# Fused attention with head mixing and a gated MLP: sooner loads of the values into a fourth buffer, one gate store split in two, two more matmul units held back

## The chip, the cores and the metric

The kernel runs on one core of one Trainium2 chip. A core has five engines with queues of their own: TensorE for matmuls (PE in the profile, its weight loads PEld), VectorE (DVE), ScalarE (ACT), GpSimd (POOL) and SyncE (SP, which here only issues DMAs). POOL issues DMAs too. The engines run independently; an instruction waits until what it needs has been signalled, and what stands behind it on the same engine waits with it. The metric is the time of one execution in microseconds (us), as the median of several runs; lower is better.

## The reference

Attention over 8 batches, 12 heads, 448 positions and head size 64, with a 12x12 mix of the heads before and after the softmax, then a two-layer MLP on all 3584 tokens (768 to 2048 to 768) whose gate is `h - tanh(h)`. Cut to what is computed:

```python
def _attn_ref(q, k, v, w_pre, w_post):
    scores = scale * np.matmul(q, k.transpose(0, 1, 3, 2))
    scores = np.einsum('bhij,hg->bgij', scores, w_pre)
    scores = scores - np.max(scores, axis=-1, keepdims=True)
    attn = np.exp(scores)
    attn = attn / (np.sum(attn, axis=-1, keepdims=True) + 1e-09)
    attn = np.einsum('bhij,hg->bgij', attn, w_post)
    return np.matmul(attn, v)

def _moe_ref(x, w_in, w_out):      # x: the 3584 x 768 result of attention
    h = x @ w_in
    g = h - np.tanh(h)
    return g @ w_out
```

## The kernel before

**Attention, about the first 860 us.** A batch is cut into four blocks of 120, 120, 120 and 88 query rows (32 blocks), and each block into groups of ten rows (45 groups a batch). The loop runs over 180 *places* `p`; each takes two groups: `premix` mixes the scores over the heads (tile `ps_p` from the gathered scores `t`), `expo` takes the maximum `mx` and the exponential `e`, `norm` makes the weights `wr` on POOL one place later, and `mix` multiplies `e` by `wr` (`ps_o`, copied to `at`). Beside that a table `todo` says which other jobs a place does: `prep_k` and `prep_q` (transposes), `scores` (`ps_q`, copied to `s`), and `values(i, t)`, which multiplies half of the heads of block `i` of the mixed attention `at` by the values `vr` (`ps_m`).

The values of a batch come in three tiles `vr` of four heads each (`hq` 0, 1, 2; 448 KB a tile). `values(i, 0)` reads tiles 0 and 1, `values(i, 1)` tiles 1 and 2. Three buffers serve all batches, so a new tile overwrites the tile with the same number of the batch before. A job `load_v(b, hq)` in the table puts the transfer on a list; at the next place SP first issues that place's gathers (`gather`, the scores `s` of two groups, read back into `t` for the place after next), and then up to six of the listed transfers, in order. Among them are also the keys `kr`, the queries `qr`, the results of attention `xs`, and the traffic of a conversion that runs beside attention: `cr` loads a piece of the MLP's weights, DVE, ACT and POOL split it, and `wi<-co`, `ss<-ct`, `wo<-co`, `ts<-ct` store it. SP is one queue: a transfer that must wait holds up all behind it.

**The MLP.** The 3584 tokens are seven blocks of 512. The first goes through plain products. The other six go in three pairs (`s` = 0, 1, 2) by a scheme that needs seven products where eight would be plain (Strassen's): `pair_step` makes seven products (`ps_h`) for one of eight pieces `q` of the hidden size, and the gates' results, in seven combinations, are stored to DRAM in `gss[s]`, slots 0 to 6, by POOL. The class `Late` does the gates of a piece in steps `v0` to `v5`, spread over the next piece's products: `v0` stores slots 0 and 1 (from `ga`), `v3` and `v4` make the second gate `gb` (the last write is the masked copy of L328), and `v5` forms the sums and stores slots 2 and 3 (from `gb`, L669) and 4 to 6 (from `gs`, L670). In `gb[:, 1]` stands the plain second gate, which is slot 3; `v5` writes only `gb[:, 0]`.

The output products are cut into *units* of twelve matmuls (`seventh`, L530 to L532: tile `y` from gates and weights). A generator (`Results.run`) yields them in a fixed order: for each `s` the slots in the order 3, 1, 6, 5, 0, 4, 2, each with `k` = 0, 2, 4, 6, and two units for each `k`. One `k` needs a gate tile of 512 KB read back from `gss[s]` (`gl<-gs`, SP, L402; in the last stretch also into free tiles such as `b22l` and `t3l`) and a weight tile of 768 KB (`w<-wo` or into `b22h`, `t4h` and others, L392 and L395). The load for `k` = 6 of any slot needs the stores of the pieces `q` = 6 and 7.

Units of one pair are mixed into the pair steps of the next (`share`). After the eighth pair step of a pair a number of units runs alone, while `Late` of the last piece is worked off, one step after every second unit (L1356 to L1367). How many is set by

```python
    HELD, AHEAD, FIRST = (14, 14, 10), (2, 4, 4), (4, 6, 5)
```

`HELD[s]` units of what was left from before are held back for that stretch, and `AHEAD[s]` units of the pair's own follow in it. After the last pair step of `s` = 2 these are 10 and 4; then the generator runs to its end with no other work beside it. The number of units in a pair step is what is left without `HELD` and `FIRST`, spread evenly.

Of the kernel before, what the change touches and what calls it, by code (L numbers as in the profile page):

```python
# [10 lines left out]
F32 = mybir.dt.float32  # L11
# [137 lines left out]
def kernel_body(  # L149
# [11 lines left out]
    nc = tc.nc  # L161
    B, H, S, D = q.shape
# [3 lines left out]
    NP = H // 2  # L166
    CP = 112
    NC = S // CP
# [29 lines left out]
    gss = [dram.tile([P, 7, NQ, TB], F32, name=f"gs{x}", tag=f"gs{x}") for x in range(NS)]  # L198
# [53 lines left out]
    def work(tag, n=2):  # L252
        return (ff.hid if tag in ("h01", "h23") else ff.rw).tile([P, n, TB], F32, name=tag, tag=tag)
# [381 lines left out]
    class Late:  # L635
# [23 lines left out]
        def v4(self):  # L659
            self.gs = work("gs", 3)  # L660
            self.g2.d4(self.gb)
            nc.vector.tensor_add(self.gs[:, 0:2], self.ga, self.gb[:, 0].unsqueeze(1).to_broadcast([P, 2, TB]))

        def v5(self):
            nc.vector.scalar_tensor_tensor(
                out=self.gs[:, 2], in0=self.ga[:, 1], scalar=-1.0, in1=self.gs[:, 0], op0=ALU.mult, op1=ALU.subtract
            )
            nc.vector.tensor_sub(self.gb[:, 0], self.gb[:, 1], self.gs[:, 2])  # L668
            nc.gpsimd.dma_start(gss[self.s][:, 2:4, self.q], self.gb)  # L669
            nc.gpsimd.dma_start(gss[self.s][:, 4:7, self.q], self.gs)  # L670
            ff.stored[self.s] = self.q + 1

# [63 lines left out]
    with ExitStack() as st:  # L736
# [7 lines left out]
        kp = st.enter_context(tc.tile_pool(name="kp", bufs=1, side="right"))  # L744
# [14 lines left out]
        def dma(dst, src, to=None):  # L759
            entry = [place[0], dst, src, None]  # L760
            (queue if to is None else to).append(entry)
            return lambda places=0: entry[3] is not None and entry[3] + places <= place[0]
# [19 lines left out]
            krs[b, hq] = t  # L782

        def load_v(b, hq):
            t = kp.tile([CP, 4, NC, D], F32, name="vr", tag="vr", bufs=3)
            sent[b, hq, "v"] = dma(
                t.rearrange("p h c d -> p h (c d)"),
                v[b, 4 * hq : 4 * hq + 4].rearrange("h (p c) d -> p h (c d)", c=NC),
            )
            vts[b, hq] = t  # L790
# [254 lines left out]
        for hq in range(3):  # L1045
            load_v(0, hq)
# [101 lines left out]
        def at_place(p, *job):  # L1148
            todo[p].append(job)

        halved = []
        for i in range(len(blocks)):
# [7 lines left out]
                    halved.append((e if i else x - 1, hi, "s", i + 1, x))  # L1160
            for x in range(2):
                halved.append(((f1 - 1) // 2 + 2, f2 // 2 + 1 if f2 < NG else NPL + 7, "v", i, x))
        at_s, p, kind = {}, 0, None
        window = {i: (lo, hi) for lo, hi, k, i, _ in sorted(halved, reverse=True) if k == "s"}
        while halved:
            ready = sorted((x for x in halved if x[0] <= p), key=lambda x: (x[1], x[3:]))
            if ready:
                x = ready[0]
                assert p <= x[1], (p, x)

                other = [y for y in ready if y[2] != kind]
                if x[2] == kind and other and x[1] > p + 1:
                    x = other[0]
                halved.remove(x)
                _, _, kind, i, n = x
                if kind == "s":
                    at_s[i, n] = p
                    for hp in (2 * n, 2 * n + 1):
                        at_place(p, scores, i, hp)
                else:  # L1180
                    at_place(p, values, i, n)
            p += 1

# [2 lines left out]
        def held(p):  # L1186
            return [a for f, *a in todo[p] if f is scores]

        for p in range(1, NPL):
            if any(f in (scores, values) for f, *a in todo[p]):  # L1190
                continue
            for of, n in ((p - 1, 1), (p + 1, 0)):
                if len(held(of)) == 2 and window[held(of)[n][0]][0] <= p <= window[held(of)[n][0]][1]:
                    i, hp = held(of)[n]
# [4 lines left out]
        for i, (b, m) in enumerate(blocks):  # L1199
            p0 = first[i] // 2  # L1200
            if i + 2 < len(blocks):
                p = at_s[i + 2, 0] - 1
                at_place(p, prep_q, i + 2, 0)
                at_place(p, prep_q, i + 2, 1)
                if i + 3 < len(blocks):
                    at_place(p + 1, load_q, i + 3)
            if b and m == 0:
                for hq in range(NP // 2):
                    at_place(p0 + 4 + hq, load_v, b, hq)
        for b in range(1, B):  # L1210
            p, o, done = first[blocks.index((b - 1, 1))] // 2 - 4, 0, []
            for hq in range(3):
                if hq == 2:

                    p = max(p, done[0] + 1)
# [107 lines left out]
    res.more_w2(2)  # L1323


    HELD, AHEAD, FIRST = (14, 14, 10), (2, 4, 4), (4, 6, 5)
    late, left = None, 4 * NQ
    for s in range(NS):
        more = s + 1 < NS
# [23 lines left out]
        n = HELD[s] + AHEAD[s]  # L1353
# [44 lines left out]
```

## Time and profile before

| | us |
|---|---|
| median of 3 runs | 1712.13 |
| lowest and highest | 1706.76, 1722.13 |
| the profiled execution | 1711.91 |
| its span, first to last instruction | 1710.2 |
| PE idle in the span (1710.2 less 1668.2 busy) | 42.0 |

The mean clock granted to TensorE over the span was 0.986. A row of the timeline gives the start, the length, the engine and line, the operation with its tiles, how many, and in brackets the idle time before it and what ended it. A row of the waits gives the engine, its line, what it waited for, the total time, how often, and the longest. A row of the windows gives a stretch, its length, the busy time of PE, PEld, DVE, ACT and POOL with the number of instructions, the granted clock (1.00 is full), the busy share of the DMA engines, and GB/s.

### The profile page before, as it was taken

To read this page: it belongs to the slowest core of one execution; us is meant where nothing else is said; L and a number is where in the kernel's file an instruction comes from. 1 tells how busy PE (TensorE), PEld (TensorE's weight loads), DVE (VectorE), ACT (ScalarE), POOL (GpSimd) and SP (SyncE) were. 2 spreads that over 40 slices of the span, in tenths; PEclk is the share of its full clock that TensorE was granted. 3 is DMA by queue.
4 is the path that set the end of the run, shared out by engine and by line. 5 is a ranking of instruction groups with operands and counts; after the bars stand their busy time and mean duration, and the time that the engine had idled before them with its cause. 6 is when DMAs were issued, how large, how long until landed. Compare 5 with 4: busy or idle time off the path is not lost.

```text
span 1710.2 us, 40889 instructions
## 1 busy us (share of the span) xinstructions
PE 1668.2 (98%) x16068; PEld 1391.2 (81%) x16068; DVE 1238.5 (72%) x1939; ACT 1091.9 (64%) x1896; POOL 601.7 (35%) x798
## 2 busy tenths in 40 slices
PE   8999999999999999999999999999999999999999
PEld 6777777777777777777787888888888888889999
DVE  5776776868868788676488799858788868778432
ACT  4776776767767677677677677565667456665331
POOL 1566575666757667563100011101001101011100
PEclk9999999999999999999999999999999999999999
DMA  8779789787887988876579899988999989988993
GB/s 190 219 233 256 228 247 266 232 253 240 247 269 231 249 252 242 253 223 210 179 260 327 291 321 311 345 300 321 321 342 352 384 272 333 320 312 327 404 413 133
DMA packets 322286, 475.06 MB, mean 278 GB/s; under 512 B 105264, under 2 KB 255280, under 8 KB 322096
## 3 DMA queue, kind: packets, MB, share of 16 engines
q1 hardware_dynamic: 305660, 414.34, 74.9%
q0 software_dynamic: 16128, 57.68, 8.7%
q8 instruction: 128, 2.10, 0.5%
q14 instruction: 62, 0.51, 0.1%
q10 hardware_dynamic: 308, 0.43, 0.1%
HBM read 274.73 MB, written 120.59 MB: 231 GB/s over the span
## 4 chain that ended last, share of the span: by engine, by line
PE 82%; DMA 9%; DVE 4%; ACT 3%; issue 2%; SPq 1%; POOL 0%; ACTq 0%; DVEq 0%; POOLq 0%
PE ps_o L955 15%; PE ps_p L918 9%; PE ps_m L997 8%; PE ps_q L874 7%; PE ps_h L289 7%; PE ps_h L290 7%; PE ps_h L292 7%; PE y L530 6%; PE y L532 6%; PE y L531 6%; DMA gl<-gs 2%; DMA t<-s 2%; DMA vr<-in_v_dram 1%; PE ps_m L840 1%; DMA wi<-co 1%
## 5 line engine op out<-in xcount | busy, mean ns | idle before, releaser
L955 PEld LDWEIGHTS ps_o<-wr,e 60*112 60x112 f32 (+1 forms) x5760 | 310.1, 177 | 33.2 <-POOL wr L938 17.4
L955 PE MATMUL ps_o<-wr,e 60*112 60x60 f32 (+1 forms) x5760 | 317.8, 261 | 8.7 <-POOL wr L938 8.0
L929 ACT ACTIVATE e<-ps_p,mx 128x448 f32<-128x448 f32 x360 | 225.3, 631 | 114.6 <-DVE mx L927 76.2
L927 DVE TENSOR_REDUCE mx<-ps_p 128x1 f32<-128x448 f32 x360 | 206.6, 615 | 88.2 <-PE ps_p L918 87.7
L965 ACT COPY at<-ps_o 112x960 f32<-112x960 f32 x156 | 153.9, 986 | 116.1 <-PE ps_o L955 115.8
L918 PE MATMUL ps_p<-t,wpre 60*64 60x448 f32 (+1 forms) x1440 | 183.1, 576 | 9.5 <-DMA t<-s 7.6
L997 PEld LDWEIGHTS ps_m<-at,vr 112*64 112x64 f32 x3072 | 150.1, 138 | 29.6 <-issue 8.0
L997 PE MATMUL ps_m<-at,vr 112*64 112x120 f32 (+1 forms) x3072 | 164.3, 264 | 6.2 <-DMA vr<-in_v_dram 6.2
L938 POOL TENSOR_TENSOR wr<-wpost,zs 128x120 f32<-128x120 f32 x180 | 69.6, 387 | 286.4 <-DVE zs L937 221.2
L530 PE MATMUL y<-w,gh 128*128 128x384 f32 x448 | 151.1, 337 | 2.3 <-issue 0.8
L531 PE MATMUL y<-w,gh 128*128 128x384 f32 x448 | 150.3, 336 | 0.0
L532 PE MATMUL y<-w,gl 128*128 128x384 f32 x424 | 143.1, 337 | 2.0 <-DVE gl L448 2.0
L874 PEld LDWEIGHTS ps_q<-kk,qh 64*120 64x120 f32 (+1 forms) x768 | 60.4, 177 | 83.5 <-issue 43.0
L874 PE MATMUL ps_q<-kk,qh 64*120 64x448 f32 (+1 forms) x768 | 124.5, 401 | 1.2 <-DVE kk L826 0.5
L669 POOL DMA_DIRECT2D gs<-gb x24 | 17.2, 718 | 292.2 <-DVE gb L668 292.2
L879 DVE COPY s<-ps_q 120x448 f32<-120x448 f32 (+1 forms) x192 | 112.4, 614 | 8.7 <-PE ps_q L874 8.4
L305 ACT ACTIVATE u<-h 128x1024 f32<-128x1024 f32 x56 | 59.5, 1063 | 74.2 <-DVE h L716 70.2
L879 ACT COPY s<-ps_q 120x448 f32<-120x448 f32 (+1 forms) x192 | 95.0, 536 | 7.0 <-PE ps_q L874 6.7
L645 POOL DMA_DIRECT2D gs<-ga x24 | 17.2, 716 | 229.6 <-DVE ga L328 222.4
L530 PEld LDWEIGHTS y<-w,gh 128*128 128x128 f32 x448 | 84.1, 188 | 7.6 <-issue 2.1
L531 PEld LDWEIGHTS y<-w,gh 128*128 128x128 f32 x448 | 84.1, 188 | 3.4
L532 PEld LDWEIGHTS y<-w,gl 128*128 128x128 f32 x424 | 79.5, 188 | 3.0 <-DVE gl L448 3.0
(371 smaller groups left out, 3987.9 us busy)
## 6 DMA issues: line engine op xcount, KB each, us to landing
t<-s SPq DMA_DIRECT2D x342, 210.0 KB
wa<-ss SPq DMA_DIRECT2D x96, 384.0 KB
w<-wo SPq DMA_DIRECT2D x43, 768.0 KB
gl<-gs SPq DMA_DIRECT2D x62, 512.0 KB
wa<-wi SPq DMA_DIRECT2D x72, 384.0 KB
w<-ts SPq DMA_DIRECT2D x35, 768.0 KB
gs<-gs POOLq DMA_DIRECT2D x24, 768.0 KB, 9.1
cr<-in_moe_w_in_dram SPq DMA_DIRECT2D x48, 256.0 KB
```

Of the source, the lines that this page charges most:

```text
L289: nc.tensor.matmul(ph, w[:, c, 0], xh, start=start and c == 0, stop=False, skip_group_check=True)
L530: nc.tensor.matmul(y, gh[:, tok], wh, start=first, stop=False, skip_group_check=True)
L531: nc.tensor.matmul(y, gh[:, tok], wl, start=False, stop=False, skip_group_check=True)
L532: nc.tensor.matmul(y, gl[:, tok], wh, start=False, stop=last, skip_group_check=True)
L874: nc.tensor.matmul(ps[:n, :S], qx[a, hp, :], kx[a, hp % 2], start=(x == 0), stop=(x == 2))
L879: eng(sts[i][:n, 2 * hp + j, :], ps[:n, :S])
L918: nc.tensor.matmul(pss[r][halves[j], :], wpre[k, :], ts[j][k, :], start=True, stop=True)
L927: nc.vector.tensor_reduce(out=mx, in_=ps, axis=AX.X, op=ALU.max, negate=True)
L929: nc.scalar.activation(e, ps, AF.Exp, bias=mx, scale=1.0, accum_out=zs[:, 0, r : r + 1])
L955: nc.tensor.matmul(ps[:CP, j, c * GP : (c + 1) * GP].rearrange("p (h i) -> p h i", i=GI)[:, :, r * GH : (r + 1) * GH], e[k, c * CP : (c + ...
L965: nc.scalar.copy(ats[i0][:, :, :, at : at + 2 * GI].rearrange("p c h (j i) -> p j (c h) i", j=2), ps[:CP, :, : NC * GP].rearrange("p j (x ...
L997: nc.tensor.matmul(pv[j * D : (j + 1) * D, r, :n], vt[:, j, c, :], ats[i][:, c, 2 * hp + j, :n], start=(c == 0), stop=(c == NC - 1),)
```

## The change

Five edits:

- `vr` has four buffers where it had three.
- The first values tile of a batch (`hq` 0) is put on the list seven places sooner (`p0 - 3` for `p0 + 4`, with `p0` the place at which the batch's first group falls). The second and third are put on it at the places of `values(i - 1, 0)` and `values(i - 1, 1)`, the last block of the batch before. To that end the planner keeps the places of `values` in `at_v`.
- The store of slots 2 and 3 is split: slot 3, `gb[:, 1]`, is stored in `v4` right after the masked copy, slot 2 in `v5` where both were.
- `HELD[2]` is 12 where it was 10.
- The scratch for DMAs whose descriptors are made in software is 2048 bytes where it was 4096.

```diff
         def v4(self):
             self.gs = work("gs", 3)
             self.g2.d4(self.gb)
+            nc.gpsimd.dma_start(gss[self.s][:, 3, self.q], self.gb[:, 1])
...
-            nc.gpsimd.dma_start(gss[self.s][:, 2:4, self.q], self.gb)
+            nc.gpsimd.dma_start(gss[self.s][:, 2, self.q], self.gb[:, 0])
...
-            t = kp.tile([CP, 4, NC, D], F32, name="vr", tag="vr", bufs=3)
+            t = kp.tile([CP, 4, NC, D], F32, name="vr", tag="vr", bufs=4)
...
-        at_s, p, kind = {}, 0, None
+        at_s, at_v, p, kind = {}, {}, 0, None
...
                 else:
+                    at_v[i, n] = p
                     at_place(p, values, i, n)
...
             if b and m == 0:
-                for hq in range(NP // 2):
-                    at_place(p0 + 4 + hq, load_v, b, hq)
+                at_place(p0 - 3, load_v, b, 0)
+                for hq in (1, 2):
+                    at_place(at_v[i - 1, hq - 1], load_v, b, hq)
...
-    HELD, AHEAD, FIRST = (14, 14, 10), (2, 4, 4), (4, 6, 5)
+    HELD, AHEAD, FIRST = (14, 14, 12), (2, 4, 4), (4, 6, 5)
...
-dynamic_dma_scratch_size=4096)
+dynamic_dma_scratch_size=2048)
```

What this does to the order of SP's queue at the second change of batch: first the rows before, from the list of SP's instructions. `vr` is a values tile, `t` the gathered scores, `kr` the keys, `qr` the queries, `xs` attention's result, `wi`, `ss` and `cr` belong to the conversion.

```order
L766 DMA kr<-in_k_dram 112x16x64
L766 DMA wi_69<-co 512x1x256
L907 DMA t<-s 120x1x448 x2
L766 DMA qr<-in_q_dram 88x12x64
L766 DMA vr<-in_v_dram 112x4x256
L907 DMA t<-s 120x1x448 x2
L766 DMA vr<-in_v_dram 112x4x256
L766 DMA xs_58<-x 768x1x208
L766 DMA ss_81<-ct 512x1x256
L766 DMA cr<-in_moe_w_in_dram 128x2x256 x2
L907 DMA t<-s 120x1x448 x2
L766 DMA vr<-in_v_dram 112x4x256
```

And the same stretch after the change (the code stands a line lower):

```order
L767 DMA vr<-in_v_dram 112x4x256
L767 DMA kr<-in_k_dram 112x16x64
L767 DMA wi_69<-co 512x1x256
L908 DMA t<-s 120x1x448 x2
L767 DMA qr<-in_q_dram 88x12x64
L908 DMA t<-s 120x1x448 x2
L767 DMA vr<-in_v_dram 112x4x256
L767 DMA xs_58<-x 768x1x208
L767 DMA ss_81<-ct 512x1x256
L767 DMA cr<-in_moe_w_in_dram 128x2x256 x2
L908 DMA t<-s 120x1x448 x2
```

The second tile now stands ahead of the keys and two pairs of gathers sooner, the third stands where the second stood, and the first is no longer in the stretch: it is thirteen rows further up in the queue.

The second place is SP's queue after the last pair step, before the change. `gs_92` is `gss[2]`, of which the first four loads are slot 3 with `k` = 0, 2, 4, 6; `wo_73` to `wo_76` are their four weight tiles.

```order
L402 DMA b11l<-gs_92 128x1024
L395 DMA t1h<-wo_73 128x2x768
L402 DMA gl<-gs_92 128x1024
L395 DMA t3h<-wo_74 128x2x768
L402 DMA gl<-gs_92 128x1024 x2
L395 DMA b22h<-wo_75 128x2x768
L395 DMA t4h<-wo_76 128x2x768
L402 DMA b22l<-gs_92 128x1024
L402 DMA t3l<-gs_92 128x1024
```

After the change:

```order
L402 DMA gl<-gs_92 128x1024
L395 DMA t3h<-wo_73 128x2x768
L402 DMA gl<-gs_92 128x1024 x2
L395 DMA b22h<-wo_74 128x2x768
L395 DMA t4h<-wo_75 128x2x768
L402 DMA b22l<-gs_92 128x1024
L402 DMA t3l<-gs_92 128x1024
L395 DMA w_19317<-wo_76 128x2x768
L395 DMA w_19319<-wo_73 128x2x768
```

Since two more units of the pair before come first, each load of `s` = 2 has moved on by one tile: the load for `k` = 6 was the second of the two `gl`, ahead of the weights for `k` = 4 and 6; it is now the one into `b22l`, behind the weights for `k` = 2 and 4 and ahead of those for `k` = 6.

POOL's queue in the same stretch has one row more for each piece; before, for the last piece (`out_dram<-c` are results that go out):

```order
L645 DMA gs_92<-ga 128x2x512
L517 DMA out_dram<-c 128x384 x4
L669 DMA gs_92<-gb 128x2x512
L670 DMA gs_92<-gs 128x3x512
L517 DMA out_dram<-c 128x384 x12
```

After:

```order
L645 DMA gs_92<-ga 128x2x512
L517 DMA out_dram<-c 128x384 x4
L662 DMA gs_92<-gb 128x512
L670 DMA gs_92<-gb 128x512
L671 DMA gs_92<-gs 128x3x512
L517 DMA out_dram<-c 128x384 x12
```

The store of slot 3 is the row L662, which waits for the masked copy and no longer for the sums; slots 2 and 4 to 6 stay where they were.

More of the change, by code (lines that the diff above doesn't have):

```diff
@@ L1380 @@
     from concourse.bass_utils import run_bass_kernel_spmd as _run
-    nc = _bacc.Bacc("TRN2", target_bir_lowering=False, num_devices=1, dynamic_dma_scratch_size=4096)
+    nc = _bacc.Bacc("TRN2", target_bir_lowering=False, num_devices=1, dynamic_dma_scratch_size=2048)
     arrays, args = {}, []
```

## Prediction

> **What bounds the kernel now.** I read the page first, then PE's waits, then the timeline of PE at its longest idle times, then windows around them with the granted clock, and last SP's queue at the same places. From the page, the span and the busy times:
>
> ```profile
> span 1710.2 us, 40889 instructions
> PE 1668.2 (98%) x16068; PEld 1391.2 (81%) x16068; DVE 1238.5 (72%) x1939; ACT 1091.9 (64%) x1896; POOL 601.7 (35%) x798
> ```
>
> PE is the bound: it idles 42.0 us in all (1710.2 - 1668.2). The change takes no matmul away, so it can only win idle time, and time that PE spends at a lower clock. Two of PE's waits, by total:
>
> ```profile
> PE ps_p L918 <- DMA t<-s: 7.6, 6, 2.7
> PE ps_m L997 <- DMA vr<-in_v_dram: 6.2, 3, 2.8
> ```
>
> The change speaks to the second, and to one wait of 2.21 us near the end. Where the longest of these fall, from PE's timeline:
>
> ```profile
> 162.98 0.98 PE L918 MATMUL ps_p<-t,wpre 60*64 60x448 f32 x8 [2.75 <-DMA t<-s]
> ...
> 265.32 1.04 PE L997 MATMUL ps_m<-at,vr 112*64 112x120 f32 x16 [1.76 <-DMA vr<-in_v_dram]
> ...
> 476.26 1.04 PE L997 MATMUL ps_m<-at,vr 112*64 112x120 f32 x16 [1.67 <-DMA vr<-in_v_dram]
> ...
> 687.62 1.04 PE L997 MATMUL ps_m<-at,vr 112*64 112x120 f32 x16 [2.76 <-DMA vr<-in_v_dram]
> ...
> 1596.66 0.41 PE L530 MATMUL y<-b22h,qb 128*128 128x384 f32 x1 [2.21 <-DMA b22h<-wo]
> ```
>
> The three waits for values come 211 us apart, at every second change of batch, 16 matmuls before the end of a `values` job: the first tile has come, the second has not. Windows around these and other places (columns as in the section on the profile):
>
> ```profile
> 264.00:276.00 12.00, 10.68 (x109) 7.96 (x110) 5.29 (x14) 4.17 (x9) 3.83 (x4) 0.72 0.90 275
> 474.00:486.00 12.00, 10.33 (x116) 8.04 (x114) 6.87 (x16) 5.96 (x14) 6.34 (x9) 0.72 0.95 298
> 686.00:698.00 12.00, 10.38 (x108) 7.82 (x108) 5.38 (x13) 4.37 (x9) 4.01 (x7) 0.72 0.92 271
> 1596.00:1604.00 8.00, 7.34 (x33) 7.37 (x34) 3.39 (x3) 2.10 (x2) 0.00 (x0) 0.79 1.03 410
> 1564.00:1594.00 30.00, 30.00 (x175) 29.87 (x174) 23.64 (x26) 13.36 (x13) 6.53 (x11) 1.00 1.02 403
> 110.00:120.00 10.00, 10.00 (x154) 8.00 (x152) 7.65 (x19) 6.92 (x17) 8.30 (x10) 1.00 0.58 206
> 245.00:275.00 30.00, 28.24 (x397) 22.27 (x392) 19.49 (x44) 17.77 (x40) 19.09 (x25) 0.89 0.96 264
> 135.00:175.00 40.00, 36.63 (x474) 28.05 (x474) 26.60 (x59) 26.16 (x61) 27.34 (x35) 0.87 0.98 277
> 355.00:395.00 40.00, 35.48 (x489) 26.36 (x486) 26.10 (x60) 25.38 (x58) 23.60 (x31) 0.96 0.94 274
> 565.00:615.00 50.00, 45.53 (x642) 34.69 (x640) 36.01 (x79) 32.48 (x74) 31.91 (x38) 0.97 0.93 257
> 1370.00:1560.00 190.00, 190.00 (x939) 170.12 (x938) 141.00 (x138) 118.55 (x139) 19.61 (x29) 1.00 0.87 302
> ```
>
> Two things are to be seen. Behind each of the four waits the granted clock drops, to 0.72 over 12 us or 0.79 over 8 us; a clock of 0.72 over 12 us loses 0.28 x 12 = 3.4 us of work, more than the wait itself. And the DMA engines are full at the changes of batch (0.93 to 0.98) but not elsewhere (0.58 at 110 to 120 us).
>
> **The fourth buffer and the sooner loads.** SP's queue at the second change of batch, the keys and the second and third tile:
>
> ```profile
> 246.66 0.65 SPq L766 DMA_DIRECT2D kr<-in_k_dram  x1
> ...
> 257.51 0.45 SPq L766 DMA_DIRECT2D vr<-in_v_dram  x1
> ...
> 265.86 0.49 SPq L766 DMA_DIRECT2D vr<-in_v_dram  x1
> ```
>
> The second tile was issued at 257.51 and let PE go on at 265.32: 7.8 us. After the change it stands ahead of the keys issued at 246.66, 10.9 us sooner, so it would land at about 254.5, while PE wants it at 265.32 - 1.76 = 263.6: 9 us to spare. The third tile takes the second's old position, lands near 265, and is wanted by the next `values`, after this one. The first goes seven places up; a place lasts about 211 / 45 = 4.7 us (two batches are 45 places and 211 us), so some 33 us. The three waits go: 1.76 + 1.67 + 2.76 = 6.2 us, and with them the three drops of the clock, 3 x 3.4 = 10.1 us. Term: **-16.3 us**.
>
> The loads that used to wait for a buffer now wait less or the same: the first finds the fourth buffer free, the second and third are issued one place after the `values` that frees theirs. Behind a waiting load stand the conversion's transfers and the next place's gathers; those gathers fill buffers of `t` that the next `premix` on PE must first read, and that `premix` stands behind the same `values` on PE. So the load never holds them longer than they are held anyway, and this wait costs nothing.
>
> What is late next at these places is the gathers and the conversion's stores, as DMA is full there. The same three windows of the odd changes of batch, which have no wait for values, show what that costs now: PE idles 40 - 36.63, 40 - 35.48 and 50 - 45.53, together 12.4 us, and loses 0.13 x 40, 0.04 x 40 and 0.03 x 50, together 8.3 us, to the clock. One of their causes, from DVE's and SP's timelines:
>
> ```profile
> 366.16 0.43 DVE L88 TENSOR_SCALAR co<-cr 128x512 int32<-128x512 int32 x1 [1.87 <-DMA wi<-co]
> ```
>
> DVE waits there for a store of the conversion to free a buffer, and PE for DVE's next step. One 448 KB tile is 1.7 us of DMA at the 275 GB/s of these windows; the change takes one or two tiles out of each full window, which may shorten those 20.7 us. But where PE no longer stands waiting at the even changes, it comes to the gathers about 5 us sooner (16.3 / 3), and the DMA has that much less time to catch up. So the bounds of this side effect are -20.7 us (all odd waits go) and +16.3 us (all that was won at the even changes comes back as waits for gathers or stores). I take 0, about the middle, since the relief of 1.7 to 3.4 us and the lost 5 us a window pull against each other.
>
> **A rule against this term.** The Trainium skill, page "TensorE: Matmul & The Clock Gate", Part 1, says the clock falls to half after an idle window of about 3.4 us, and its list of rules asks only for no idle gaps over about 3 us. By that, gaps of 1.67 to 2.76 us would cost no clock at all, and removing them would bring only the idle time. The trace differs: each of the four has its drop in the row of its window. The measurement decides; what the rule would make of the time stands among the rivals.
>
> **The tail: two more units held, the store split.** SP's queue after the last pair step, and the steps around it on PE, DVE, POOL and ACT:
>
> ```profile
> 1573.34 16.74 SPq L402 DMA_DIRECT2D gl<-gs  x2
> 1590.18 0.52 SPq L395 DMA_DIRECT2D b22h<-wo  x1
> ```
>
> ```profile
> 1562.98 0.33 PE L530 MATMUL y<-w,gh 128*128 128x384 f32 x1
> ...
> 1577.12 1.39 DVE L328 COPY_PREDICATED gb<-gs,t 128x1024 f32<-128x1024 int32 x1
> ...
> 1582.73 0.71 POOL L669 DMA_DIRECT2D gs<-gb  x1 [11.83 <-DVE gb L668]
> ...
> 1594.64 1.04 ACT L442 CAST t<-gl 128x1024 fp32r<-128x1024 f32 x1 [4.11 <-DMA gl<-gs]
> ```
>
> The second of the two `gl` is slot 3, `k` = 6; it waits for the store that POOL issues at 1582.73, until about 1590. The weights `b22h` of `k` = 4 stand behind it, are issued at 1590.18, and PE waits 2.21 us for them at 1596.66. After the change `b22h` and `t4h` stand ahead of that load, and are the weights of `k` = 2 and 4. Behind it stand the weights of `k` = 6. A unit is 12 matmuls, 12 x 30 / 175 = 2.06 us (row 1564 to 1594). From the first unit at 1562.98 one unit of the last pair step and 16 held ones come before `k` = 4 and two more before `k` = 6, which starts 19 x 2.06 = 39.1 us later; before it was two units less. The store of slot 3 can go when the masked copy ends, at 1577.12 + 1.39 = 1578.5, 4.2 us before 1582.73. So its data, which were ready for ACT 1594.64 - 1562.98 = 31.7 us after the first unit, come at 27.5 us, and the weights behind, at 6.5 us from issue like `b22h`, at about 1590.18 + 6.5 + 1 - 4.2 - 1563.0 = 30.5 us. Both have 8 us to spare; without the split they would still have 4. So the wait goes, 2.21 us, and its clock, 0.21 x 8 = 1.7 us. Term: **-3.9 us** (bounds 0, if another weight tile comes late instead, and -3.9).
>
> **What costs nothing.** Two units leave the pair steps of the last pair. In the row 1370 to 1560 PE is busy for all 190.0 us and DVE for 141.0, so the steps are set by PE, and 4 us less of it leaves DVE (141 of 186) still under it; if that cover were gone, at most the 4.1 us moved would come back as waits. The 24 more DMA issues on POOL go by
>
> ```profile
> L669 POOL DMA_DIRECT2D gs<-gb x24 | 17.2, 718 | 292.2 <-DVE gb L668 292.2
> ```
>
> 718 ns each, where POOL waits 292 us in all: 24 x 0.72 = 17.2 us under that idle time, with no one behind them but stores. If they weren't hidden, one Late step's 0.72 us would delay the last stores, which have 4 us or more. The halved scratch has no row. Below, it cannot be a gain, since no transfer changes; above, POOL could at worst hold a store until an earlier one has landed, and in the tail that has the spare of 8 us. I take 0.
>
> **Sum.** Against the profiled execution's own time, 1711.9 us (span 1710.2): 1711.9 - 16.3 - 3.9 + 0 = **1691.7, given as 1692 us**. The median of the runs shown, 1712.13, is 0.2 above the profiled execution.
>
> **The rivals.** (1) *The waits come back as others.* The gathers or the conversion's stores stop PE at the even changes of batch. For it: DMA at 0.96 from 245 to 275 us, and t<-s already a wait of 7.6 us in all. Against it: the loads leave that stretch. Half back gives 1692 + 8 = 1700, all back 1708. (2) *The odd changes are relieved as well.* For it: two of their three values loads leave the full stretch. Half of 20.7 us gives 1682, all 1671. (3) *Only the idle time is won*, the clock drops having causes of their own: 1711.9 - 6.2 - 2.2 = 1703.5. Against it stand four drops at four waits. By the page named above the time would be this one. (4) *Slower: the moved loads make gathers late where they now go.* A wait like the one at 162.98 costs 2.75 us and, with 0.13 x 40 = 5.2 us of clock, 7.9 us. It decides from five such new waits on (the 20.2 won and 17.1 beyond): 1692 + 39.5 = 1731. For it: the stretch from 135 us on is as full (0.98). Against: 110 to 120 us, toward which a first tile moves, is at 0.58, and PE has no wait where the loads stand sooner in the rows above. (5) *The change does not do what it says*, some load being held as long as before: 1712.
>
> **How the numbers follow.** Likeliest, 1692 with a range of its own of 1685 to 1698: 0.40. Rival 2: 0.24. Rival 1: 0.23. Rival 3: 0.06. Rival 4: 0.05. Rival 5: 0.02. A measurement of this kernel can tell about 1% from no change, 17 us, so faster means under 1695.0: 0.30 of the likeliest and all of rival 2, 0.54. Slower means over 1729.2: 0.04 of rival 4. Within 1%: the rest, 0.42. The range that holds 8 in 10 is 1676 to 1708: it leaves out the far half of rival 2, rival 4 and rival 5.
>
> **What would show it.** Right: no wait of PE for `vr`; windows at 264, 474 and 686 us (a little sooner) at a clock near 1.00; SP held at the load for `k` = 6 for some 4 us less than 16.7, with no wait of PE for `b22h`; the store of L662 about 4 us ahead of L670. Wrong: new waits of PE for `t<-s` or `wr` between 245 and 275 us and at the two later places (rival 1); fewer waits from 135 to 175, 355 to 395 and 565 to 615 us (rival 2); drops of the clock at those places without a wait (rival 3).

## The result, and the profile after

| | before | after |
|---|---|---|
| median of 10 runs each, us | 1711.65 | 1700.10 |
| lowest and highest | 1706.76, 1722.13 | 1693.54, 1704.79 |
| the profiled execution | 1711.91 | 1702.99 |
| its span | 1710.2 | 1701.0 |

The ratio of after to before is 0.9927, with a 95% interval of 0.9908 to 0.9945: the changed kernel is faster by 0.7%, and the interval stays clear of 1. (Of the kernel before, one more execution, timed beside the last three experiments, took 2742.23 us at a mean clock of 0.546 and is left out of every ratio and spread.) The gain is 11.6 us in the medians and 8.9 us in the two profiled executions, against 20.2 us foretold. From the page after, the span and the busy times:

```profile
span 1701.0 us, 40968 instructions
PE 1663.0 (98%) x16068; PEld 1389.2 (82%) x16068; DVE 1239.5 (73%) x1939; ACT 1090.6 (64%) x1896; POOL 612.2 (36%) x822
```

PE idles 38.0 us where it idled 42.0. So 4.0 of the 9.2 us between the two spans are idle time; the other 5.2 us are matmuls that took less time, that is, clock. PE's waits after, by total:

```profile
PE ps_o L956 <- POOL wr L939: 9.2, 9, 3.9
PE ps_p L919 <- DMA t<-s: 6.1, 3, 2.6
PE y L530 <- DMA w<-wo: 3.5, 3, 1.2
PE ps_q L875 <- DVE x L1016: 3.2, 2, 1.6
```

The wait for `vr` is gone and so is the one for `b22h`, as foretold. In their place the list has a line that was not there: PE waits for VectorE's copy into `x`. Where it falls, from PE's timeline after (the other rows are the longest waits at the odd changes of batch, and two in the MLP):

```profile
361.61 3.25 PE L956 MATMUL ps_o<-wr,e 60*112 60x60 f32 x32 [3.92 <-POOL wr L939]
...
474.54 0.67 PE L875 MATMUL ps_q<-kk,qh 64*120 64x448 f32 x3 [1.58 <-DVE x L1016]
...
476.33 2.14 PE L956 MATMUL ps_o<-wr,e 60*112 60x60 f32 x32 [0.92 <-POOL wr L939]
...
576.01 1.27 PE L919 MATMUL ps_p<-t,wpre 60*64 60x448 f32 x8 [2.62 <-DMA t<-s]
...
684.34 0.67 PE L875 MATMUL ps_q<-kk,qh 64*120 64x448 f32 x3 [1.62 <-DVE x L1016]
...
686.09 3.25 PE L956 MATMUL ps_o<-wr,e 60*112 60x60 f32 x32 [0.88 <-POOL wr L939]
...
1336.18 0.41 PE L530 MATMUL y<-w,gh 128*128 128x384 f32 x1 [1.22 <-DMA w<-wo]
...
1341.80 0.41 PE L530 MATMUL y<-w,gh 128*128 128x384 f32 x1 [1.22 <-DMA w<-wo]
```

474.54 and 684.34 are the second and third of the even changes, where PE stood for values before, and 476.33 and 686.09 what follows from them (VectorE's late sums, and so POOL's weights `wr`). 361.61 and 576.01 are odd changes. Windows over all six changes after, the even ones first:

```profile
245.00:275.00 30.00, 28.77 (x416) 22.11 (x414) 19.38 (x46) 18.51 (x41) 18.37 (x24) 0.94 0.95 261
455.00:485.00 30.00, 26.43 (x354) 20.23 (x352) 18.73 (x40) 16.58 (x37) 17.83 (x22) 0.89 0.93 262
665.00:705.00 40.00, 37.50 (x504) 29.27 (x504) 24.88 (x56) 23.43 (x54) 22.47 (x26) 0.87 0.85 229
135.00:175.00 40.00, 39.81 (x597) 30.74 (x594) 30.64 (x71) 29.42 (x67) 29.13 (x38) 1.00 0.98 284
355.00:395.00 40.00, 36.08 (x480) 27.47 (x480) 25.10 (x57) 25.98 (x61) 24.14 (x31) 0.91 0.88 257
565.00:615.00 50.00, 46.92 (x656) 35.92 (x650) 36.52 (x80) 34.43 (x78) 33.28 (x42) 0.97 0.84 253
```

And the two windows of before that the prediction did not show:

```profile
455.00:485.00 30.00, 28.33 (x404) 22.41 (x404) 21.05 (x49) 19.26 (x43) 20.09 (x24) 0.89 0.99 267
665.00:705.00 40.00, 37.24 (x539) 29.21 (x537) 26.01 (x60) 23.47 (x53) 24.03 (x29) 0.91 0.96 257
```

In each row the loss is the length less PE's busy time, and the length times what the clock lacks to 1.00. Added over the three even and the three odd windows (`e4` is an experiment below):

| us lost: idle + clock | before | after | e4_third_later |
|---|---|---|---|
| three even changes | 6.2 + 10.2 = 16.4 | 7.3 + 10.3 = 17.6 | 1.8 + 0 = 1.8 |
| three odd changes | 12.4 + 8.3 = 20.7 | 7.2 + 5.1 = 12.3 | 9.5 + 6.7 = 16.2 |

So the even changes, for which the loads were moved, lose as much as before; the odd ones lose 8.4 us less. The part behind attention is 4.4 us shorter (1.7 of it is a drop of the clock at the end of attention that the profile before has and the one after does not). Together with the even changes (+1.2) that is 11.6 us; the remaining 2.4 us, to the 9.2 between the spans, were lost between these windows (a wait for gathers at 53 us drew a drop of the clock that it did not draw before).

A profile is one execution, and these sums differ from one to the next. The experiments below give more of them, with the same windows:

| us lost (of it idle) | three even changes | three odd changes |
|---|---|---|
| loads at the old places: before, e2, e5, e6, e9, e11 | 10.1 to 16.4 (6.2 to 7.3) | 15.5 to 21.7 |
| attention as changed: after, e1 | 17.6 and 8.9 (7.3 and 5.3) | 12.3 and 16.5 |
| `x` in halves: e3 | 10.8 (7.2) | 15.1 |
| third tile later: e4, e7, e8, e10 | 1.8 to 2.6 (1.8 to 2.6) | 11.5 to 16.2 |

At the even changes the idle time hardly moved with the change, and the means of the two groups, 12.8 and 13.3 us, are alike; the profile before is the highest of its six. At the odd changes the means are 19.3 and 14.4 us, so 8.4 us is more than the change gives there on average.

What PE waits for at the even changes stands in VectorE's timeline after:

```profile
260.78 0.81 DVE L1016 COPY x<-ps_m 128x360 f32<-128x360 f32 x1 [2.15 <-DMA xs<-x]
...
360.31 0.43 DVE L88 TENSOR_SCALAR co<-cr 128x512 int32<-128x512 int32 x1 [3.85 <-DMA wi<-co]
...
473.71 0.78 DVE L1016 COPY x<-ps_m 128x360 f32<-128x360 f32 x1 [2.06 <-DMA xs<-x]
...
683.51 0.77 DVE L1016 COPY x<-ps_m 128x360 f32<-128x360 f32 x1 [3.87 <-DMA xs<-x]
```

Two blocks of a batch share one tile `x`, and there is one buffer for it. The copy for the next block, after `values`, waits until the store `xs<-x` of the tile before (624 KB here) has landed. VectorE stands still in the meantime, and PE waits because its next scores `ps_q` go into the PSUM buffers that the values `ps_m` use, which this copy frees. (360.31 is the odd change: there a store of the conversion holds VectorE for 3.85 us, and PE's 3.92 us at 361.61 are its consequence.) SP's queue after shows what stands ahead of the store:

```profile
465.71 0.47 SPq L767 DMA_DIRECT2D vr<-in_v_dram  x1
466.28 0.69 SPq L767 DMA_DIRECT2D xs<-x  x1
```

The store is issued right behind the third tile of values and lets VectorE go on at 473.71, 7.4 us later. The prediction's price for what is late next missed this wait, though it stood in the profile before; VectorE's waits and timeline there:

```profile
DVE x L1015 <- DMA xs<-x: 8.1, 3, 3.3
```

```profile
267.29 0.79 DVE L1015 COPY x<-ps_m 128x360 f32<-128x360 f32 x1 [2.69 <-DMA xs<-x]
...
479.02 0.78 DVE L1015 COPY x<-ps_m 128x360 f32<-128x360 f32 x1 [2.14 <-DMA xs<-x]
...
689.51 0.78 DVE L1015 COPY x<-ps_m 128x360 f32<-128x360 f32 x1 [3.26 <-DMA xs<-x]
```

Each ends 1.9 to 2.8 us after PE's wait for values (265.32, 476.26, 687.62). Two waits lay beside each other; the change took away the one that PE showed.

### The profile page after: what moved, and what is told of

Same layout as the page of the kernel before. It is cut to its first block, busy times and chain, and to the rows that moved or that the text cites. A ratio compares the mean times of both kernels' runs of the same rounds, so it can differ in the third digit from the quotient of the medians.

```text
span 1701.0 us, 40968 instructions
## 1 busy us (share of the span) xinstructions
PE 1663.0 (98%) x16068; PEld 1389.2 (82%) x16068; DVE 1239.5 (73%) x1939; ACT 1090.6 (64%) x1896; POOL 612.2 (36%) x822
## 4 chain that ended last, share of the span: by engine, by line
PE 83%; DMA 6%; DVE 4%; ACT 3%; issue 2%; SPq 1%; POOL 0%; ACTq 0%; DVEq 0%; POOLq 0%
PE ps_o L956 14%; PE ps_m L998 9%; PE ps_p L919 9%; PE ps_h L292 7%; PE ps_h L289 7%; PE ps_h L290 7%; PE ps_q L875 7%; PE y L530 6%; PE y L532 6%; PE y L531 6%; DMA t<-s 2%; DMA w<-wo 2%; PE ps_m L841 1%; DMA xs<-x 1%; PE ps_m L815 1%
## 5 line engine op out<-in xcount | busy, mean ns | idle before, releaser
L998 PEld LDWEIGHTS ps_m<-at,vr 112*64 112x64 f32 x3072 | 155.0, 142 | 23.0 <-issue 8.5
L998 PE MATMUL ps_m<-at,vr 112*64 112x120 f32 (+1 forms) x3072 | 168.6, 268 | 0.0
L530 PE MATMUL y<-w,gh 128*128 128x384 f32 x440 | 148.4, 337 | 4.0 <-DMA w<-wo 3.5
L531 PE MATMUL y<-w,gh 128*128 128x384 f32 x440 | 147.6, 336 | 0.0
L645 POOL DMA_DIRECT2D gs<-ga x24 | 17.5, 728 | 242.9 <-DVE ga L328 242.9
L442 ACT CAST gh<-gl 128x1024 fp32r<-128x1024 f32 x60 | 62.5, 1042 | 27.3 <-DMA gl<-gs 16.0
```

Of the source, the lines that this page charges most:

```text
L530: nc.tensor.matmul(y, gh[:, tok], wh, start=first, stop=False, skip_group_check=True)
L531: nc.tensor.matmul(y, gh[:, tok], wl, start=False, stop=False, skip_group_check=True)
L998: nc.tensor.matmul(pv[j * D : (j + 1) * D, r, :n], vt[:, j, c, :], ats[i][:, c, 2 * hp + j, :n], start=(c == 0), stop=(c == NC - 1),)
```

## The experiments

The theory after the result: the gain of the values is real, but at the even changes the wait for `x` (a store of 7.4 us behind a tile of 448 KB) takes its place. The rival: DMA is full there, so that any wait taken away comes back as another (gathers, conversion). Beside that the two parts had to be priced apart. All were timed against the kernel before on the same chip (its medians there: 1713.46 us for the first four runs, 1712.52 for the next four, 1711.52 for the last three).

| label | median us | ratio to before, 95% interval |
|---|---|---|
| e1_values_only | 1700.68 | 0.9929, 0.9904 to 0.9954 |
| e2_tail_only | 1713.15 | 1.0003, 0.9980 to 1.0027 |
| e3_x_halves | 1696.55 | 0.9912, 0.9885 to 0.9940 |
| e4_third_later | 1694.60 | 0.9902, 0.9876 to 0.9928 |
| e5_split_only | 1710.43 | 0.9991, 0.9971 to 1.0011 |
| e6_held_only | 1707.24 | 0.9985, 0.9967 to 1.0002 |
| e7_third_no_split | 1693.78 | 0.9909, 0.9879 to 0.9940 |
| e8_third_co3 | 1691.83 | 0.9888, 0.9863 to 0.9913 |
| e9_buffer_only | 1709.70 | 0.9981, 0.9959 to 1.0003 |
| e10_no_split_co3 | 1694.07 | 0.9888, 0.9852 to 0.9924 |
| e11_scratch_only | 1711.94 | 0.9988, 0.9963 to 1.0014 |

### One part at a time

**e1_values_only**, the changed kernel without the tail's two edits:

```diff
-            nc.gpsimd.dma_start(gss[self.s][:, 3, self.q], self.gb[:, 1])
...
-            nc.gpsimd.dma_start(gss[self.s][:, 2, self.q], self.gb[:, 0])
+            nc.gpsimd.dma_start(gss[self.s][:, 2:4, self.q], self.gb)
...
-    HELD, AHEAD, FIRST = (14, 14, 12), (2, 4, 4), (4, 6, 5)
+    HELD, AHEAD, FIRST = (14, 14, 10), (2, 4, 4), (4, 6, 5)
```

> The fourth buffer, the sooner loads and the halved scratch alone; the store in one piece and 10 units held as before. Theory A: the change won 3.9 us at the tail and the rest, 11.6 - 3.9 = 7.7 us of the medians, in attention, because at the even changes of batch the wait for values only gave way to DVE's wait for the store xs<-x. The parts then add up: 1711.7 - 7.7 = 1704.0 us, ratio 0.9955, no wait of PE for vr, and the wait of 2.2 us for b22h near the end back. Rival B: the tail's part is larger or smaller than its 3.9 us since attention leaves it in another state; then this run lies outside 1702 to 1706.

It has all of the change's gain: 0.9929 against 0.9927. So the expected 1704 us (0.9955) was wrong, and the rival holds: in the time the tail's part is nothing that can be seen. PE waits for no `vr`, and the tail's wait is back, from PE's timeline:

```profile
1585.40 0.53 PE L530 MATMUL y<-b22h,qb 128*128 128x384 f32 x1 [2.24 <-DMA b22h<-wo]
```

**e2_tail_only**, the kernel before with only the tail's edits (three buffers, old places, old scratch):

```diff
+            nc.gpsimd.dma_start(gss[self.s][:, 3, self.q], self.gb[:, 1])
...
-            nc.gpsimd.dma_start(gss[self.s][:, 2:4, self.q], self.gb)
+            nc.gpsimd.dma_start(gss[self.s][:, 2, self.q], self.gb[:, 0])
...
-    HELD, AHEAD, FIRST = (14, 14, 10), (2, 4, 4), (4, 6, 5)
+    HELD, AHEAD, FIRST = (14, 14, 12), (2, 4, 4), (4, 6, 5)
```

> The split store and 12 held units alone; three value buffers, old places of the loads, scratch of 4096. Theory A: 1711.7 - 3.9 = 1707.8 us, ratio 0.9977; PE's three waits for vr stand as before (about 6.2 us), the wait for b22h is gone, and nothing takes its place. Rival B: another weight tile or gate tile comes late instead, and the ratio is 0.999 to 1.001.

No gain: 1.0003, and the 0.9977 of the theory lies just outside the interval. The wait for `b22h` is gone here too, but another has grown; PE's waits:

```profile
PE ps_m L998 <- DMA vr<-in_v_dram: 5.1, 3, 2.4
PE y L530 <- DMA w<-wo: 2.8, 3, 1.3
```

PE waits for weights (`w<-wo`) at 1346 and 1352 us, 0.99 and 1.34 us; before, the idle times there were 0.34 us without a DMA behind it and 0.61 us for ACT. The changed kernel has the two rows of 1.22 us shown above. Which of the two edits gives and which takes was the next question.

**e5_split_only** and **e6_held_only**, the kernel before with one of the two:

```diff
+            nc.gpsimd.dma_start(gss[self.s][:, 3, self.q], self.gb[:, 1])
...
-            nc.gpsimd.dma_start(gss[self.s][:, 2:4, self.q], self.gb)
+            nc.gpsimd.dma_start(gss[self.s][:, 2, self.q], self.gb[:, 0])
```

```diff
-    HELD, AHEAD, FIRST = (14, 14, 10), (2, 4, 4), (4, 6, 5)
+    HELD, AHEAD, FIRST = (14, 14, 12), (2, 4, 4), (4, 6, 5)
```

> Kernel before with the second gates' plain slice stored apart alone; three tiles of values, ten units held. Theory A (the term for the tail is right and needs the split): ratio to before about 0.998, no wait for b22h near 1590 us. Theory B (the wait goes by the two held units, and the store adds transfers while the units read their weights): the wait for b22h stays near 2.2 us, the waits for w<-wo near 1340 us are 2 to 3 us in all as in the changed kernel (0.6 to 0.9 us of idle time there before), ratio 0.999 to 1.002.

> Kernel before with two more units held alone; three tiles of values, one store of both slices. Theory A: the wait for b22h stays or only moves, ratio 0.999 to 1.001. Theory B: the wait for b22h near 1590 us is gone and the waits for w<-wo near 1340 us stay below 1.5 us in all, ratio about 0.997 to 0.999.

PE's waits, first with the split alone, then with the units alone:

```profile
PE y L530 <- DMA w<-wo: 2.5, 2, 1.7
...
PE y L530 <- DMA b22h<-wo: 1.4, 1, 1.4
```

```profile
PE y L530 <- DMA w<-wo: 0.5, 1, 0.5
```

The held units take the wait for `b22h` away by themselves. The split alone only shortens it from 2.2 to 1.4 us. Beside it stand waits for `w<-wo` of 2.5 us, where the held units alone have 0.5 us. These weights are not late by the split alone, though: at the two units near 1340 us (1326 to 1357 us over all profiles) PE's waits for `w<-wo` come to 2.3 to 3.1 us in the six profiles with the split and to 0 to 2.0 us in the seven without it (1.6 in e11, which differs from the kernel before only in the scratch). On average the split adds some 1.6 us. The times do not show it, since all three intervals hold a ratio of 1 and lie over one another. Why the store apart would make the weights late is not shown: it moves no byte more, but POOL issues it at 1328.73 us, 3.7 us ahead of slot 2 at 1332.44, among the loads of these weights, and DMA is full there (1.00 busy from 1300 to 1350 us, in the kernel before, after, and in e6).

### What holds the even changes

**e3_x_halves**: `x` in two tiles of half the heads, each stored as soon as it is copied (the temporary of the first keys moves to a `vr` buffer, since `x` no longer has its size).

```diff
-            x = kp.tile([P, NP * 2 * MT + LINE], F32, name="x", tag="x", bufs=1)
+            x = kp.tile([P, NP * MT + LINE // 2], F32, name="x", tag=f"x{t}", bufs=1)
...
-                if t == 1 and (m % 2 or m == NM - 1):
-                    dma(xs[b][:, :, starts[m0] : starts[m] + n], xt[i][:, :, : off + n])
+                if m % 2 or m == NM - 1:
+                    dma(xs[b][:, 3 * t : 3 * t + 3, starts[m0] : starts[m] + n], xt[i, t][:, :, : off + n])
...
-            load_k(0, hq, kp.tile([CP, NC, 4, D], F32, name="tmp_k", tag="x", bufs=1) if hq == 2 else None)
+            load_k(0, hq, kp.tile([CP, NC, 4, D], F32, name="tmp_k", tag="vr", bufs=4) if hq == 2 else None)
```

> The changed kernel, with the tile x (attention's result before it is stored) cut into two tiles of three head pairs, each stored as soon as its own half of values is copied; so the first half's store goes out two places sooner, and the next batch's first copy waits for that half only. The bytes are the same, 16 stores are now 32. Theory A: DVE's wait for xs<-x at the even changes (8.1 us in three waits) goes, and with it PE's waits of about 6 us and their drops of the clock of about 10 us: 5 to 14 us below the changed kernel, 1686 to 1695 us. Rival B: DMA is full there, so the gathers or the conversion's stores stop PE instead: within 3 us of the changed kernel, 1697 to 1703 us.

VectorE waits for no `xs<-x` any more, and the median, 1696.55, is 3.6 us below the changed kernel's, between the two ranges expected. But at the even changes PE idles 7.2 us, as in the changed kernel (7.3). Its longest waits there are now for the conversion (1.63 us), for gathers (1.44) and, at the third of them, for POOL's weights, since VectorE is held by a store of the conversion there, where it was held 3.87 us by `xs<-x`; VectorE's row, then PE's:

```profile
681.42 0.43 DVE L88 TENSOR_SCALAR co<-cr 128x512 int32<-128x512 int32 x1 [4.47 <-DMA wo<-co]
```

```profile
682.72 3.24 PE L956 MATMUL ps_o<-wr,e 60*112 60x60 f32 x32 [2.26 <-POOL wr L939]
```

Over the whole kernel PE's waits for gathers rise from 6.1 to 10.0 us:

```profile
PE ps_p L919 <- DMA t<-s: 10.0, 7, 2.9
```

So the rival is right about the wait for `x` taken alone: the idle time comes back as waits for other transfers. At the third change the third tile still stands ahead of both stores: SP issues it at 672.30 us, `xs<-x` at 673.28 and `wo<-co` at 673.80.

**e4_third_later**: the changed kernel with the third tile of values one place later, behind `xs<-x` and not ahead of it.

```diff
                 for hq in (1, 2):
-                    at_place(at_v[i - 1, hq - 1], load_v, b, hq)
+                    at_place(at_v[i - 1, hq - 1] + hq - 1, load_v, b, hq)
```

> The changed kernel, with the third values tile put on the list one place later, so that it stands behind xs<-x and the conversion's transfers on SP and no longer right ahead of them. Theory A: xs<-x lands about one 448 KB tile sooner, 1.7 us, and DVE's waits for xs<-x (3.9 us at most) and for the conversion's stores behind it shrink by that: 3 to 8 us below the changed kernel, 1692 to 1697 us. Rival B (DMA full, the order within the stretch does not matter): within 3 us, 1697 to 1703 us. A third tile that now comes late would show as a wait of PE for vr.

1694.6 us, in the theory's 1692 to 1697. SP's queue, then VectorE's timeline, then the windows of the even changes:

```profile
464.13 0.58 SPq L767 DMA_DIRECT2D xs<-x  x1
...
466.86 0.85 SPq L767 DMA_DIRECT2D vr<-in_v_dram  x1
```

```profile
470.37 0.80 DVE L1016 COPY x<-ps_m 128x360 f32<-128x360 f32 x1
```

```profile
245.00:275.00 30.00, 29.24 (x446) 22.43 (x440) 20.24 (x50) 20.43 (x44) 19.31 (x27) 1.00 0.95 265
455.00:485.00 30.00, 29.03 (x442) 22.22 (x442) 21.62 (x50) 20.38 (x45) 18.75 (x24) 1.00 0.97 284
665.00:705.00 40.00, 39.98 (x586) 30.90 (x586) 31.03 (x69) 27.96 (x63) 27.99 (x35) 1.00 0.91 279
```

The store stands ahead of the tile, the copy 6.2 us behind its issue no longer waits (nor do those of the other two even changes by more than 1.0 us), the clock is at 1.00 in all three windows, and they lose 1.8 us where they lost 16.4 before the change. The other three versions with the third tile later (below) lose 1.8 to 2.6 us there, each at a clock of 1.00 in all three windows. DMA is as full as ever (0.91 to 0.97): it was the order of the transfers, not the amount. In e4 the tile stands behind `xs<-x` and two gathers, and at two of the three changes behind a store of the conversion as well, so which of these had to go first is not separated; by e3 it is not `xs<-x` alone. The rival holds for a small part: PE's waits for `t<-s` are 9.4 us, but in eleven pieces of at most 1.7 us.

**e9_buffer_only**: the kernel before with four buffers and half the scratch, the loads at the old places.

```diff
-            t = kp.tile([CP, 4, NC, D], F32, name="vr", tag="vr", bufs=3)
+            t = kp.tile([CP, 4, NC, D], F32, name="vr", tag="vr", bufs=4)
```

> Kernel before with a fourth buffer for the tiles of values and half the scratch, the loads at the places of before. If the fourth buffer alone relieves the even changes (the third load of a batch waited for a buffer), the waits for vr fall from 5 to 6 us to below 2 and the ratio is 0.993 to 0.996. If the loads' places are what counts (my theory: they are issued too late, not held by a buffer), the waits for vr stay at 4 to 6 us and the ratio is 0.999 to 1.001.

The waits for values stand, so no load was held by a buffer; the places count:

```profile
PE ps_m L997 <- DMA vr<-in_v_dram: 6.0, 3, 2.9
```

Its ratio, 0.9981, has an interval that holds 1 and allows a small gain; that the buffer brings nothing at all is not shown by the time. Whether the sooner places would do with three buffers was not run.

**e11_scratch_only**: half the scratch and nothing else.

```diff
-dynamic_dma_scratch_size=4096)
+dynamic_dma_scratch_size=2048)
```

> Kernel before with half the scratch for software DMA descriptors and nothing else. The term at nothing is right: ratio 0.999 to 1.001, POOL's DMA issues near 718 ns each. Rival: POOL has to wait for descriptors to be used up, its issues grow by tens of ns or more at the tail, and the ratio is 1.002 or more.

No effect that can be measured. The group of POOL's stores is as before (718 ns):

```profile
L669 POOL DMA_DIRECT2D gs<-gb x24 | 17.2, 719 | 291.1 <-DVE gb L668 291.1
```

### Versions that go further

**e7_third_no_split** is e4 with the store of both slices joined again:

```diff
-            nc.gpsimd.dma_start(gss[self.s][:, 3, self.q], self.gb[:, 1])
...
-            nc.gpsimd.dma_start(gss[self.s][:, 2, self.q], self.gb[:, 0])
+            nc.gpsimd.dma_start(gss[self.s][:, 2:4, self.q], self.gb)
```

> The changed kernel with the third tile of values loaded one place later and without the separate store. If the store apart gives back what the held units win (theory B of the tail), this one lies 1 to 3 us below the version with the store apart: 1692 to 1694 us, ratio 0.989. If the store is needed (theory A), it lies 2 to 4 us above: 1696 to 1699, with the wait for b22h back.

1693.78 us, 0.8 below e4, and no wait for `b22h`: the split is not needed. Whether it costs time can't be told at this size.

**e8_third_co3** is e4 with a third buffer for the conversion's `co`; **e10_no_split_co3** is e7 with the same:

```diff
-    o = pool.tile([p, 4, 2, 128], F32R, name="co", tag="co", bufs=2)
+    o = pool.tile([p, 4, 2, 128], F32R, name="co", tag="co", bufs=3)
```

> The changed kernel with the third tile of values one place later and a third buffer for the converted tiles co. If VectorE's waits for the stores wi<-co and wo<-co (3.8 to 5.3 us each in the changed kernel) still hold TensorE up, the waits for wr (7.7 us in all with two buffers) fall to 3 to 5 us and the time lies 3 to 8 us below: 1687 to 1692 us. If the 16 DMA engines are what is short (0.9 and more busy at the changes of batch), the waits move to other places and the time is that with two buffers, 1693 to 1697.

> The changed kernel with the third tile of values one place later, without the separate store, and a third buffer for the converted tiles co. If these three add up (0.8 us for the store, 2.8 us for the buffer in the medians so far): 1690 to 1692 us, ratio 0.987 to 0.989. If the DMA engines are what is short and the buffer only moves waits to the gathers: 1692.5 to 1695, ratio 0.989 to 0.991.

PE's waits in e8:

```profile
PE ps_p L919 <- DMA t<-s: 14.3, 11, 2.7
...
PE ps_o L956 <- POOL wr L939: 3.0, 6, 1.2
```

The third buffer does what it says: VectorE has no wait for `wi<-co` or `wo<-co` left, and PE's wait for `wr` falls from 7.7 to 3.0 us. But the waits for gathers rise by 4.9 us, from 9.4 to 14.3. The medians, 1691.83 and 1694.07, lie on either side of e7, and the ratios are both 0.9888. Here the rival is right in the traces: what is relieved comes back as gathers; in the times a gain of the third buffer can't be told from none. All four versions with the third tile later (e4, e7, e8, e10) beat both kernels in the median, by 5.5 to 8.3 us against the changed one. Each one's interval overlaps that of the change. Taken together their 24 runs average 1694.0 us, and the 19 runs of the changed kernel and e1, which have the same attention, 1700.1 us, each with a standard error of 1.0 us, on chips where the kernel before averages 1711.5 to 1713.0: a gain of 6 us, clear of the noise.

## Why the prediction was right or wrong

**Direction and range.** 1700.1 us lies in 1676 to 1708, and the sign was right. The likeliest, 1692, with its own range of 1685 to 1698, was not: the kernel came out where rival 1 with "half back" stood, 1700. That is luck: nothing came half back. In the two profiles the even changes gave nothing and the odd ones gave 8.4 us for which nothing was put down. Faster by over 1% had 0.54; the ratio of 0.9927 is within 1%.

**The term of -16.3 us failed at "what is late next".** The loads did what was worked out: the tiles come in time and PE waits for no `vr`. What came next was named as gathers and the conversion's stores; it was VectorE's copy into the one buffer of `x`, which waits for `xs<-x`. With that wait gone as well (e3), gathers and the conversion's stores came next, as named. The prediction put this at 0; at the even changes it took all. They gave 0 (16.4 us lost before, 17.6 after) and not 16.3. What they can give e4 shows, with the third tile behind the store: 16.4 to 1.8, so 14.6 us in these two profiles. But the size was taken from an execution at the high end: the six profiles with the loads at the old places lose 12.8 us there on average, of it 6.2 to the clock (3.6 to 10.2) and not 10.1, since behind 8 of their 18 long waits for values (1.0 to 2.9 us) the clock did not fall. The mean of the four with the later tile is 2.2, so the size is rather 10.6 us, an estimate from these means. The wait for `x` could have been read in the profile before: 8.1 us in VectorE's list, at the same three places. The step that was left out is to ask, at each place where a wait goes, for the next instruction on every other engine there that waits for a DMA, and when that ends.

**Rival 1** happened at the even changes, in full, with the store of `x` first, and gathers and the conversion's stores behind it (e3).

**Rival 2, the odd changes**, happened at the same time: 20.7 us lost before, 12.3 after. All of it, in these two profiles, is the first of them, where the wait of 2.75 us at 162.98 us and its 5.2 us of clock are gone; the window's losses fell from 8.6 to 0.2 us. In the six profiles with the loads at the old places (before, e2, e5, e6, e9, e11) PE waits 1.5 to 3.1 us there; in the five with the new places and two `co` buffers (after, e1, e3, e4, e7) it waits for gathers 1.4 us in e1, 1.0 us in e7 and not in the other three. With three `co` buffers (e8, e10) the wait is back, 2.7 and 2.9 us, so this gain hangs on what else DMA has to do there. The other two odd changes were not relieved in a way that holds over the kernels. The prediction took these side effects at 0, between -20.7 and +16.3: they were -8.4 at the odd changes, less than half of that bound, and +17.5 at the even ones (1.2 + 16.3), a little past the other, +9.1 together.

**Rival 3, idle time only**, falls. In e4 the clock went from 0.89, 0.89 and 0.91 to 1.00 at the even changes when the waits there went, and it is 1.00 there in e7, e8 and e10 too. The Trainium skill, page "TensorE: Matmul & The Clock Gate", Part 1, asks for idle windows of about 3.4 us before the clock falls. The traces here differ, and decide: they show drops behind waits of 1.6 to 2.8 us.

**Rivals 4 and 5** did not happen. No row shows gathers late in five new places, and the loads moved as written.

**The tail's -3.9 us** was right for its own wait in the trace, and no time shows it: no wait for `b22h`, the load for `k` = 6 let go early, but e2's ratio is 1.0003. SP's queue and POOL's stores after:

```profile
1567.00 0.52 SPq L395 DMA_DIRECT2D t4h<-wo  x1
1575.84 0.33 SPq L402 DMA_DIRECT2D b22l<-gs  x1
```

```profile
1570.06 0.54 POOL L662 DMA_DIRECT2D gs<-gb  x1 [3.91 <-DVE gb L328]
1573.77 0.54 POOL L670 DMA_DIRECT2D gs<-gb  x1 [3.17 <-DVE gb L669]
```

The store of slot 3 is 3.7 us ahead of slot 2 (4.2 foretold), and the load into `b22l` follows it at 1575.84. But "without the split they would still have 4 us" was the sentence to act on: e6 shows that the two units alone suffice. And the split was costed on POOL, at nothing, and not at the end of the pair before: 2.4 us of waits for weights near 1340 us, against 0.95 us of idle time before. That is 1.5 us more, and some 1.6 us by the means of all profiles. Net of that the term is about -2.4 us, which no run here can tell from 0. The prediction called DMA full at the changes of batch and not elsewhere; its own rows from 1564 and 1596 us have it at 1.02 and 1.03, so the MLP was a place to look too.

**What was costed at nothing.** POOL's issues: one store of two slices took 718 ns, two of one slice take 554 and 549 ns, so 24 x 0.385 = 9.2 us more where 17.2 were put down, all under idle time. The scratch: nothing (e11).

## What to carry to other kernels

Before pricing a wait that goes, list the waits of every engine within a few us of its end, not only those of the engine that is the bound: an in-order engine may have a second wait beside it, which becomes the first the moment the other goes. In a queue where DMA is full, look at which transfer stands ahead of those that somebody will wait for: the versions with one tile moved one place back gain 6 us here (1700.1 to 1694.0 us over 19 and 24 runs), while taking away one engine's wait (e3) only handed the idle time to others. Do not price a drop of the clock from one profile. And try the parts of an edit alone: two that were aimed at the same wait were one too many.

## What the hardware showed that was not expected

The clock of TensorE falls after waits much shorter than thought, but not after each. In the thirteen profiles, the share of PE's waits after which the granted clock of the next 12 us was below 0.95:

| PE's wait, us | in attention (60 to 850 us) | in the MLP |
|---|---|---|
| 0.6 to 1 | 12 of 31 | 0 of 38 |
| 1 to 1.5 | 21 of 52 | 4 of 43 |
| 1.5 to 2 | 17 of 23 | 3 of 8 |
| 2 and more | 22 of 23 | 2 of 2 |

The waits come in clusters in attention, so some drops in the first two rows belong to a neighbour. The drops have steps: 0.86, 0.72 and 0.57 over 12 us are 1.7, 3.4 and 5.2 us of work lost. Cut into stretches of 0.85 us, two of the longest are stretches at half the clock: behind the waits at 162.98 us before and 684.34 us after it reads 0.50 for some 10 us, and 1.00 ahead of that and behind it. The same wait of 1.19 us at the end of attention (at 852 us before, at 847 us after) was followed by 0.86 in the one and 1.00 in the other. The runs of each kernel here spread over 8 to 21 us, and their mean clocks go with it: in e2 the fastest run took 1704.51 us at 0.989, the slowest 1724.27 us at 0.980, a difference in clock of 0.009 or some 15 us of such a span.
